# A feed-forward block by one level of Strassen, its weights prepared in seven pieces, and a planner with new figures

## The chip, the core and the metric

The kernel runs on one core of a Trainium2 chip. The core has a matrix engine (TensorE, PE in the profile, with its weight loads as PEld), a vector engine (VectorE, DVE), a scalar engine (ScalarE, ACT), a general engine (GpSimd, POOL) and a queue that starts most transfers (SyncE, SP). The metric is the time of one execution on the device in microseconds; lower is better.

## What is computed

Three layers stand behind each other, for 2304 tokens (4 sequences of 576) of width 512:

```python
# attention, 8 heads of width 64, seq 576, a bias from the positions
scores = q @ k.T / sqrt(64) + bias          # bias: a small two-layer net on log distances
attn = exp(scores - max); attn = attn / sum
x = attn @ v                                 # (2304, 512)
# first feed-forward, 512 -> 2048 -> 512
h = x @ w_in;  x = (s * relu(h)**2 + b) @ w_out
# second feed-forward, 512 -> 2048 -> 512
h = x @ w_in2; out = (h - tanh(h)) @ w_out2
```

The feed-forward weights arrive as 64-bit floats.

## The kernel before

Every operand of a large product is scaled by a power of two and split into two 16-bit floats, a high part and a low part. A product is then three matmuls (high by high, high by low, low by high) that add up in PSUM. Making a high part is one scaled copy (line 488 on VectorE or line 490 on ScalarE), a low part one scalar_tensor_tensor on VectorE (line 493). A 64-bit weight first becomes a 32-bit float by three integer operations on VectorE (lines 1101, 1104 and 1107), on pieces of 128 by 1024.

The attention runs in 144 units of 128 query rows by 576 keys: scores on TensorE (line 911), bias and maximum on VectorE (943), exp on ScalarE (953), high part (965 or 963), low part on GpSimd (971), a transposing DMA, and the product with the values (990, 996). The first feed-forward takes the tokens in 9 blocks of 256: 16 chunks of hidden units (1406), relu and square on ScalarE, high part (1429) on VectorE, low part on GpSimd (1433), then the output product (1475) into a single PSUM bank that is emptied (1489, 1494) before the next column group can start. It is mixed with the attention on TensorE's queue and goes on after the attention's end.

Once the last transposed attention output is stored, the attention's memory is freed (the task `turn`), and the weights of the second feed-forward are loaded through two staging buffers (`w2raw`), converted, and split into `w2big`. The second feed-forward takes a first block of 256 tokens and four of 512: for each of 16 hidden chunks twelve matmuls (`pg`, 1707), tanh on ScalarE (1715), h - tanh on VectorE (1719), high part (1726) and low part (493) on VectorE, then for each of four output columns 48 matmuls (`pq`, 1755), a scaled copy on ScalarE (1767), and a store.

The order on each engine's queue is fixed when the program is built. A planner (`Schedule`) plays the tasks through with a cost for each task and engine, takes for each free engine the task with the lowest due number among those that can start, and where a task has several engines, the one it comes to first. The table `SHIFT` moves the due numbers of groups of tasks.

## Time and profile before

| | |
|---|---|
| runs | 1095.21, 1097.35, 1097.79 us; median 1097.35 |
| profiled execution: span from the first to the last instruction | 1094.4 us |
| the runs' median less the span, the part that lies around it | 2.95 us |
| TensorE busy | 993.5 us (91%), 9231 matmuls |
| VectorE busy | 735.4 us (67%), 1551 instructions |
| ScalarE busy | 554.1 us (51%) |
| GpSimd busy | 339.1 us (31%) |
| mean granted TensorE clock | 0.964 of 2.4 GHz |

The page gives the profiled execution's span; its own time is taken as that span and the 2.95 us. Busy times of one engine are ends of instructions less their starts, and neighbours overlap a little, so the pace of an engine is read from start to start. A matmul's shown duration holds its way through the array as well; its pace, too, is the distance between starts.

### The profile page before, as it was taken

The page shows a single profiled execution, that of the slowest core. Times are in us where ns is not written, and L with a number is a line of the kernel's source. Part 1 is how long each engine was busy: PE and PEld are TensorE (multiplying, and loading weights), DVE is VectorE, ACT ScalarE, POOL GpSimd, SP SyncE. Part 2 cuts the span into 40 slices and gives each one's busy share as a digit, 9 for nine tenths or more (in the row PEclk, how much of TensorE's full clock was granted, in tenths as well). Part 3 has the DMA queues.
Part 4 walks back from the last instruction along what each step waited for, and adds up shares of the span by engine and source line. Part 5 has one row for each costly group of instructions (what it writes and reads, how often), then busy time and mean ns, then how long its engine had stood idle before and what let it go on. Part 6 is the DMA issues. An engine that isn't in the chain of part 4 may idle for free. (4 is left out here: it accounts for less than half of the span.)

```text
span 1094.4 us, 23536 instructions
## 1 busy us (share of the span) xinstructions
PE 993.5 (91%) x9231; PEld 668.8 (61%) x9234; DVE 735.4 (67%) x1551; ACT 554.1 (51%) x1120; POOL 339.1 (31%) x371
## 2 busy tenths in 40 slices
PE   6547677999998899999999999999999999999998
PEld 3113245678787677878778788887454444444443
DVE  6999999945677686877773689998852487016200
ACT  6898878768776665665655365631220122102100
POOL 6035346545475375656744041400000000000000
PEclk9767888999999999999999999999999999999999
DMA  9979996799999799999896644412000000000000
GB/s 342 369 209 233 252 264 114 179 234 220 245 169 220 157 219 182 191 157 195 156 180 118 205 146 169 159 54 92 1 5 20 20 1 1 20 20 6 15 29 29
DMA packets 250368, 153.10 MB, mean 140 GB/s; under 512 B 197392, under 2 KB 216464, under 8 KB 250256
## 3 DMA queue, kind: packets, MB, share of 16 engines
q1 hardware_dynamic: 250256, 151.59, 58.3%
q8 instruction: 72, 1.18, 0.5%
q14 instruction: 40, 0.33, 0.1%
...
## 5 line engine op out<-in xcount | busy, mean ns | idle before, releaser
L971 POOL TENSOR_TENSOR hl<-e,hl 128x64 f16<-128x64 f32 (+1 forms) x288 | 230.2, 821 | 240.9 <-ACT hl L965 145.0
L1475 PE MATMUL po<-hr,w1big 128*128 128x256 f16 x1728 | 202.4, 273 | 11.2 <-ACT x L1494 7.7
L1755 PE MATMUL pq<-w1big,w2big 128*128 128x512 f16 (+1 forms) x960 | 189.5, 358 | 0.0
L1475 PEld LDWEIGHTS <-w1big 128*128 128x128 f16 x1728 | 165.7, 98 | 35.3 <-issue 16.5
L1406 PEld LDWEIGHTS <-w1big 128*128 128x128 f16 x1728 | 165.8, 99 | 31.4 <-issue 11.7
L1707 PE MATMUL pg<-hr,w2big 128*128 128x512 f16 x768 | 168.0, 379 | 0.0
L1755 PEld LDWEIGHTS <-w2big 128*128 128x128 f16 x960 | 93.8, 98 | 92.6
L1707 PEld LDWEIGHTS <-w2big 128*128 128x128 f16 x960 | 93.8, 98 | 92.5
L953 ACT ACTIVATE e<-sp,mx 128x576 f32<-128x576 f32 x144 | 105.5, 733 | 57.6 <-DVE mx L947 37.0
L943 DVE CUSTOM_DVE_ANT_0 sp<-sp,bi 128x576 f32<-128x576 f32 x144 | 109.7, 761 | 33.9 <-PE sp L911 24.3
L1433 POOL TENSOR_TENSOR hr<-r,hr 128x512 f16<-128x512 f32 x72 | 93.3, 1297 | 117.8 <-DVE hr L1429 106.0
L1715 ACT ACTIVATE t<-pg,ich 128x512 f32<-128x512 f32 (+1 forms) x80 | 51.4, 644 | 142.7 <-PE pg L1707 136.8
L1719 DVE SCALAR_TENSOR_TENSOR t<-pg,ich,t 128x512 f32<-128x512 f32 (+1 forms) x80 | 55.2, 695 | 100.1 <-ACT t L1715 99.8
L1406 PE MATMUL ph<-xt_own,w1big 128*128 128x256 f16 x960 | 115.2, 276 | 3.8 <-DMA xt_own<-xh 2.3
L911 PE MATMUL sp<-ks,qs 64*128 64x288 f16 (+1 forms) x960 | 83.4, 298 | 24.4 <-ACT e L953 22.7
L1767 ACT ACTIVATE o<-pq,osc 128x512 f32<-128x512 f32 (+1 forms) x20 | 12.9, 644 | 161.8 <-PE pq L1755 161.8
L1406 PE MATMUL ph<-w1big 128*128 128x256 f16 x768 | 89.1, 274 | 0.0
L965 ACT ACTIVATE hl<-e 128x576 f16<-128x576 f32 x110 | 74.7, 679 | 24.1 <-DMA et<-hl 22.2
L911 PEld LDWEIGHTS <-qs 64*128 64x128 f16 (+1 forms) x960 | 47.5, 100 | 49.9 <-issue 37.5
L990 PEld LDWEIGHTS <-et 128*128 128x128 f16 (+1 forms) x1440 | 54.3, 103 | 36.8 <-issue 20.2
L990 PE MATMUL xp<-vp,et 128*128 128x64 f16 (+1 forms) x1440 | 65.1, 198 | 12.3 <-DMA et<-hl 8.8
L1429 DVE CAST hr<-r 128x512 f16<-128x512 f32 x72 | 41.2, 574 | 29.2 <-ACT r L1424 24.3
...
## 6 DMA issues: line engine op xcount, KB each, us to landing
...
```

The costliest lines, as they stand in the source:

```text
L911: nc.tensor.matmul(out=out, lhsT=qs.tile[64 * h:64 * h + 64, sq, p * r:p * r + r], rhs=ks.tile[64 * h:64 * h + 64, sk, half * HS:(half + 1 ...
L943: nc.vector.tensor_tensor_reduce(out=st, in0=st, in1=bi.tile.rearrange("p (a b) -> p a b", a=2), scale=-1.0 / KAP, scalar=3.0e38, op0=ALU. ...
L953: nc.scalar.activation(out=put(e, row_tile("e")).rearrange("p (a b) -> p a b", a=2), in_=sp.tile[:, :, 0:HS], func=AF.Exp, scale=-1.0, bia ...
L965: nc.scalar.activation(out=h[:, 0:S], in_=e.tile, func=AF.Copy)
L971: nc.gpsimd.tensor_tensor(out=hl.tile[:, o:o + m], in0=e.tile[:, c:c + m], in1=hl.tile[:, c:c + m], op=ALU.subtract)
L990: nc.tensor.matmul(out=xp[r0:r0 + r, o:o + 64], lhsT=et.tile[:, n, r0:r0 + r], rhs=vp.tile[:, 0, n % 5, 64 * h:64 * h + 64], start=n == 0, ...
L1406: nc.tensor.matmul(out=ph.tile[:, fi, :], lhsT=win_ap(1, sw, m, f), rhs=xa(sx, m), start=m == 0 and j == 0, stop=m == KM - 1 and j == 2,)
L1433: nc.gpsimd.tensor_tensor(out=rh[:, :, 1, :], in0=r.tile, in1=rh[:, :, 0, :], op=ALU.subtract)
L1475: nc.tensor.matmul(out=po.tile[:, :NB1], lhsT=wout_ap(1, sw, f, c), rhs=rhl[f // 8][:, f % 8, sr, :], start=f == 0 and j == 0, stop=f == K ...
L1707: nc.tensor.matmul(out=pg.tile[:, :n], lhsT=win_ap(2, sw, m, f), rhs=xh[:, sx, m, :n], start=m == 0 and i == 0, stop=m == KM - 1 and i == 2,)
L1719: nc.vector.scalar_tensor_tensor(out=tt.tile[:, :n], in0=pg.tile[:, :n], scalar=xs2[j][1], in1=tt.tile[:, :n], op0=ALU.mult, op1=ALU.subtract,
L1755: nc.tensor.matmul(out=pq.tile[:, :n], lhsT=wout_ap(2, sw, f, c), rhs=g[:, sr, :n], start=f == 0 and i == 0, stop=f == KF - 1 and i == 2,)
```

## The change

The second feed-forward is computed by one level of Strassen's method (in the form with seven products and fifteen sums). Tokens are in 9 blocks of 256, the 2048 hidden units in two slices of 1024, so there are 18 rounds `k`. In each round, the input product (128 + 128 tokens, 256 + 256 input columns, 512 + 512 hidden units) takes seven products `in_product(k, p)` and the output product seven `out_product(k, p)`, each of 24 matmuls with a 128-wide moving operand and a weight load each, where plain blocks would take eight. The sums are formed on VectorE: on the weights (`wsum`, line 1753), on the block's input (`xsum`, 1820), on the hidden values (`add`, `combine`; 1968 to 2031) and on the output (2091 to 2137). High and low parts are now needed for seven sums where there were four quarters. The tables `ONLY` and `opts` keep all of these off GpSimd.

The weights are loaded into seven staging places that are later overwritten, are converted at once (eight pieces of the input weights, then eight of the output weights, four of these in two halves of 128 by 512), and are then split; before, conversion, splitting and the first block's work were mixed. The planner gets other costs per task, another rule for VectorE beside GpSimd, other costs for transfers, and a new `SHIFT`, so that every queue's order is new, in the attention as well. In the attention, 49 of the 144 high parts stand on VectorE (before 34) and 95 on ScalarE (before 110).

```diff
--- before
+++ after
+EARLY, E0, EP = 0, 40, 50
-AHEAD = 3.4
+AHEAD = 6.0
+COST = {
+    "u.ex@act": 1.056, "u.hi@act": 1.132, "bias.lambda@act": 1.102, "f.relu@act": 0.952, "f.square@act": 1.145,
...
+}
+PORT = {"u.ttr": 0.0, "x.scale": 0.0, "scan.add": 0.0, "k.lambda": 0.4, "v.lambda": 0.4, "q.lambda": 0.4, "s.lambda": 0.4,
...
+}
+ONLY = {"I.fn": "dve", "I.sub": "dve", "J.fn": "dve", "J.c22": "dve", "I.add": "dve", "X.xsum": "dve", "P.wsum": "dve", "u.lo": "pool", "f.lo": "pool"}
-    ".begin": -153, ".identity": -9.52, ".fn": -349.02, ".lambda": 99.24, "scan0.lambda": -15.42, "scan0.fn":
...
+    ".begin": -932.5, ".fn": 1185, ".lambda": 1257, "I0.add": -102.8, "I0.fn": -1616, "I0.lambda": -1827.5,
...
-    HOP = 0.23
-    PACE = dict(pe=1.0, act=1.02, dve=1.06, pool=1.0)
-    DMA_START, DMA_DONE = 0.65, 2.0
+    HOP = dict(pe=0.22, act=0.07, dve=0.07, pool=0.1, turn=0.0)
+    LATE = dict(act=0.034, dve=0.034, pool=0.034)
+    OVER = dict(act=0.1, dve=0.085, pool=0.04)
+    DMA_START, DMA_DONE = 1.2, 0.65
+    SHARE, SHARE_POOL, SHARE_MAX = 0.65, 0.18, 2.1
...
+                if eng == "dve" and t.share > 0.0:
+                    rest = port["pool"] - at
+                    if rest > 0.0:
+                        cost = min(cost + t.share * rest, cost * self.SHARE_MAX)
+                        late("pool", self.SHARE_POOL * min(rest, cost))
+                    port["dve"], user["dve"] = at + cost, t
+                elif eng == "pool":
+                    rest = min(port["dve"] - at, cost)
+                    if rest > 0.0:
+                        cost += self.SHARE_POOL * rest
+                        late("dve", user["dve"].share * rest)
+                    port["pool"], user["pool"] = at + cost, t
+                free[eng] = at + max(cost - self.OVER[eng], 0.06)
+                t.end = at + cost + self.LATE[eng]
...
-    def w2_f32(i):
-        return (big2[0][:, i + 1, :] if i < 7 else w1big[:, 5, :]).bitcast(F32)
-
...
+    PC = 2048
+    ORD_IN, ORD_OUT = (1, 2, 5, 6, 3, 7, 4), (1, 5, 2, 3, 7, 6, 4)
+    XSLOT = {1: 0, 2: 1, 3: 3, 4: 6, 5: 4, 6: 5, 7: 2}
+    HT = NB1 // 2
...
+    def w2_late(i, j, deps, prio, dest=()):
...
+        if g == 0:
+            bufs = [lambda: flat2(big2[0][:, 2 * n % 14:2 * n % 14 + 2, :]).bitcast(U32)]
+        elif n % 2 == 0:
+            bufs = [lambda: w1big[:, 5, :].bitcast(U32)]
+        else:
+            bufs = [lambda: f_pc(22).bitcast(U32), lambda: xt_own[:, 1, :].bitcast(U32)]
+        war = [x for x in t_stage.get((g, n - (2 if g else 7)), [])]
...
+    def w2_split(g, s, deps, prio):
+
+        sc.tag = f"P{g}{s}"
+        i1, i2 = 4 * g + s, 4 * g + s + 2
+        if g == 0:
+            q = {11: (i1, 0), 12: (i1, 1), 21: (i2, 0), 22: (i2, 1)}
+        else:
+            q = {11: (i1, 0), 12: (i2, 0), 21: (i1, 1), 22: (i2, 1)}
+        raw = {k: (lambda v=v: raw2(*v)) for k, v in q.items()}
+
+        def split(p, src, deps, o):
+            dst = lambda part: prod_w(g, s, p)[:, part].rearrange("p a n -> p (a n)")
+            th = sc.add(
+                {ACT: 1.14}, lambda e: copy_scale(dst(0), src(), w2s["c", g], e), deps + [t_w2c[g]], prio + o
+            )
+            tl = sc.add({DVE: 1.28}, lambda _: low_part(dst(1), src(), w2s["c", g], dst(0)), [th], prio + o + 0.5)
+            t_wp[g, s, p] = [th, tl]
+            return [th, tl]
+
+        def combine(out, a, b, op, deps, o):
+            def wsum(e):
+                (nc.gpsimd if e == POOL else nc.vector).tensor_tensor(out=out(), in0=a(), in1=b(), op=op)
+            return [sc.add({POOL: 2.5, DVE: 1.21}, wsum, deps, prio + o)]
+        a22 = split(4, raw[22], deps, 0)
+        a11 = split(1, raw[11], deps, 1)
+        a12 = split(2, raw[12], deps, 2)
+        s1 = combine(raw[22], raw[21], raw[22], ALU.add, a22, 0)
+        split(5, raw[22], deps + s1, 3)
+        s3 = combine(raw[21], raw[11], raw[21], ALU.subtract, s1, 1)
+        split(7, raw[21], deps + s3, 5)
+        s2 = combine(raw[11], raw[22], raw[11], ALU.subtract, s3 + a11, 1)
+        split(6, raw[11], deps + s2, 4)
+        s4 = combine(raw[12], raw[12], raw[11], ALU.subtract, s2 + a12, 2)
+        split(3, raw[12], deps + s4, 6)
+        return [x for p in PRODS for x in t_wp[g, s, p]]
...
+        def combine(out, i, j, op, deps):
+            def xsum(e):
+                x = x_raw()
+                (nc.gpsimd if e == POOL else nc.vector).tensor_tensor(out=x[:, out], in0=x[:, i], in1=x[:, j], op=op)
+            return sc.add({POOL: 0.95, DVE: 0.37}, xsum, deps, prio)
+        t1 = combine(4, 2, 0, ALU.subtract, lds + [t])
+        t3 = combine(2, 3, 2, ALU.subtract, [t1])
+        t2 = combine(5, 3, 4, ALU.subtract, [t1])
...
+    def in_product(k, p):
...
+            w = prod_w(0, s, p)
+            xs = y()[:, :, XSLOT[p]].rearrange("p s (m n) -> p s m n", m=2)
+            for f in range(4):
+                for m in range(2):
                     for i, (sw, sx) in enumerate(((0, 0), (0, 1), (1, 0))):
                         nc.tensor.matmul(
-                            out=pg.tile[:, :n], lhsT=win_ap(2, sw, m, f), rhs=xh[:, sx, m, :n],
-                            start=m == 0 and i == 0, stop=m == KM - 1 and i == 2,
+                            out=bank.tile[:, f * HT:(f + 1) * HT], lhsT=w[:, sw, m, f * 128:(f + 1) * 128], rhs=xs[:, sx, m],
...
+        def split(n, q):
+            i = st["G", n]
+            dst = lambda part: g_mem[k % 2]()[:, (q - 1) * 1024 + part * 512:(q - 1) * 1024 + part * 512 + 512]
+            war = [t_prod["out", k - 2, q]] if k >= 2 else moe1_end if k == 0 else out_done[1]
+            o = pr + 100 + 10 * ORD_OUT.index(q)
+            th = sc.add(
+                {ACT: 0.72, DVE: 0.49}, lambda e: copy_scale(dst(0), i.tile, names["cg"], e), [st["tG", n]] + war, o, [], [i]
+            )
...
+        if p == 1:
+            copy("E1", bank)
+        elif p == 2:
+            gate(11, st["E1"], [from_psum("E1", bank)])
+            split(11, 1)
+        elif p == 5:
+            copy("E5", bank)
+        elif p == 6:
+            copy("E2", bank)
+        elif p == 3:
+            gate(12, st["E2"], [from_psum("E2", bank)])
+            combine("T1", 12, 11)
+            split("T1", 5)
+        elif p == 7:
+            copy("E3", bank)
+            e3, e5 = st["E3"], st["E5"]
+
+            def add(e):
+                eng_of(e).tensor_tensor(out=e3.tile, in0=e3.tile, in1=e5.tile, op=ALU.add)
+            tc22 = sc.add(dual(add), add, [st["t", "E3"], st["t", "E5"]], pr, [], [e3, e5])
+            gate(22, e3, [tc22])
+            combine("T3", 22, 12)
+            combine("T2", 22, "T1")
+            split(22, 3)
+            split("T3", 7)
+            split("T2", 6)
+        else:
+            gate(21, bank, [t], True)
+            combine("T4", 21, "T2")
+            split(21, 2)
+            split("T4", 4)
+
+    accs = {}
+
...
+    def out_product(k, p):
...
+            w = prod_w(1, s, p)
+            g = g_mem[k % 2]()[:, (p - 1) * 1024:p * 1024].rearrange("p (s k n) -> p s k n", s=2, k=4)
+            o = (j % 2) * 256
+            for f in range(4):
+                for c in range(2):
+                    for i, (sw, sx) in enumerate(((0, 0), (0, 1), (1, 0))):
+                        nc.tensor.matmul(
+                            out=bank.tile[:, o + c * HT:o + (c + 1) * HT], lhsT=w[:, sw, f, c * 128:(c + 1) * 128],
+                            rhs=g[:, sx, f], start=new and f == 0 and c == 0 and i == 0,
+                            stop=s == 1 and f == 3 and i == 2, skip_group_check=True,
+                        )
...
+    NS = 2 * NB2
+    for k in range(NS + 1):
+        if k < NS and k % 2 == 0 and k // 2 + 1 < NB2:
+            pass
+        ins = [(in_product, k, p) for p in ORD_IN] if k < NS else []
+        outs = [(out_product, k - 1, p) for p in ORD_OUT] if k else []
+        order = ins
+        if ins and outs:
+            order = ins[:3] + outs[:1] + ins[3:4] + outs[1:2] + ins[4:5] + outs[2:3] + ins[5:6] + outs[3:5] + ins[6:] + outs[5:]
+        elif outs:
+            order = outs
+        for fn, kk, p in order:
+            fn(kk, p)
+        if k % 2 == 0 and k // 2 + 1 < NB2:
+            prep_tasks(k // 2 + 1, 1e4 + 200 * (k + 1) - 300)
     sc.run()
 
```

VectorE's queue around the first block of the second feed-forward. `xs`/`am` (before) and `cols` (after) belong to that block's scales, `hr<-r` to the first feed-forward, `w2raw` is a staging buffer; in the new order `w1big` and `xt_own` are staging, too. Before:

```order
L1107 SCALAR_TENSOR_TENSOR w2big<-w2raw,w2big 128x1024
L1608 TENSOR_REDUCE am<-xs 128x4
L1615 TENSOR_REDUCE sx<-am 128x1
L1616 TENSOR_TENSOR am<-am,w2r_ic 128x4
L1617 TENSOR_REDUCE sx<-am 128x1
L493 SCALAR_TENSOR_TENSOR w2big<-w2big,w_c 128x1024
```

After:

```order
L1178 SCALAR_TENSOR_TENSOR w2big<-w1big,w2big 128x1024
L1500 CAST hr<-r 128x2x256
L1172 TENSOR_SCALAR w2big<-w2big 128x512
L1172 TENSOR_SCALAR w2big<-xt_own 128x512
L1175 SCALAR_TENSOR_TENSOR w2big<-w2big 128x512
L1175 SCALAR_TENSOR_TENSOR w2big<-xt_own,w2big 128x512
L1178 SCALAR_TENSOR_TENSOR w2big<-w2big 128x512
L1500 CAST hr<-r 128x2x256
L1178 SCALAR_TENSOR_TENSOR w2big<-xt_own,w2big 128x512
L1788 TENSOR_REDUCE cols<-w1big 128x8
```

Before, the block's first reduction stood behind 9 of the 16 conversions and ahead of all splitting; now it stands behind all 16 conversions and behind the splits and sums of all the input weights.

The same queue a little later, behind that block's low parts (`w1big<-w2big,w_c,w1big` is a low part of an output weight, L1753 a sum of weights, `pb` a PSUM bank of the first round). After:

```order
L563 SCALAR_TENSOR_TENSOR w1big<-w1big,cols 128x1280
L563 SCALAR_TENSOR_TENSOR w1big<-w2big,w_c,w1big 128x1024 x2
L1753 TENSOR_TENSOR w2big<-w2big 128x1024
L563 SCALAR_TENSOR_TENSOR w1big<-w2big,w_c,w1big 128x1024
L1753 TENSOR_TENSOR w2big<-w2big 128x1024
L563 SCALAR_TENSOR_TENSOR w1big<-w2big,w_c,w1big 128x1024
L1753 TENSOR_TENSOR w2big<-w2big 128x1024
L563 SCALAR_TENSOR_TENSOR w1big<-w2big,w_c,w1big 128x1024
L1753 TENSOR_TENSOR w2big<-w2big 128x1024
L563 SCALAR_TENSOR_TENSOR w1big<-w2big,w_c,w1big 128x1024
L1968 SCALAR_TENSOR_TENSOR w2big<-pb,cols,w2big 128x512
L563 SCALAR_TENSOR_TENSOR w1big<-w2big,w_c,w1big 128x1024
```

The first round's first result from PSUM (L1968) is taken in between the output weights' low parts; before, the first block's hidden values were worked off in between conversions.

TensorE's queue where the second feed-forward begins (`po` is the first feed-forward's output, `pg` and `pa` hidden values of the second). Before:

```order
L1475 LDWEIGHTS w1big
L1475 MATMUL po<-hr,w1big 128x256
L1707 LDWEIGHTS w2big
L1707 MATMUL pg<-xt_own,w2big 128x256
```

After:

```order
L1546 LDWEIGHTS w1big
L1546 MATMUL po<-hr,w1big 128x256
L1942 LDWEIGHTS w2big
L1942 MATMUL pa<-w1big,w2big 128x128
```

Each matmul has a weight load of its own in both. Before, the first `pg` stood behind 636 of the 1068 matmuls of the first feed-forward that follow the attention's last product; now the first `pa` stands behind 1080 of 1176; 108 of these matmuls, which stood ahead of the attention's last product, stand behind it now.

## Rows read from the trace of the kernel before

**Rows 1.** Busy time by stage; columns: stretch, length, each engine's busy time (instructions), clock, DMA

```profile
core 0: us, PE busy (x) PEld busy (x) DVE busy (x) ACT busy (x) POOL busy (x), PEclk, DMA share, GB/s
27.00:220.00 193.00, 133.36 (x1350) 74.44 (x1351) 184.30 (x353) 160.10 (x309) 79.75 (x80) 0.81 0.89 231
220.00:591.00 371.00, 349.80 (x4684) 290.53 (x4684) 255.63 (x696) 245.37 (x542) 210.51 (x260) 1.00 0.98 191
591.00:640.00 49.00, 46.43 (x445) 41.23 (x438) 27.04 (x41) 23.17 (x52) 10.14 (x10) 1.00 0.52 170
640.00:740.00 100.00, 96.47 (x878) 85.51 (x877) 95.36 (x154) 51.80 (x106) 21.60 (x13) 1.00 0.38 130
740.00:1094.00 354.00, 350.58 (x1712) 166.98 (x1709) 155.44 (x267) 56.63 (x84) 0.00 (x0) 1.00 0.06 20
```

**Rows 2.** Chain that ended last, in order of time; columns: start, length, what

```profile
716.36 5.24 PE po L1475 x48
...
756.20 41.44 PE pg L1707 x192
...
1090.62 0.03 ACTq L1767
```

**Rows 3.** Groups of instructions by line and shape; busy time, mean ns, idle before

```profile
L1707 PE MATMUL pg<-hr,w2big 128*128 128x512 f16 x768 | 168.0, 379 | 0.0
L1755 PE MATMUL pq<-w1big,w2big 128*128 128x512 f16 x768 | 167.9, 379 | 0.0
...
L1707 PEld LDWEIGHTS <-w2big 128*128 128x128 f16 x960 | 93.8, 98 | 92.5
...
L1707 PE MATMUL pg<-xt_own,w2big 128*128 128x256 f16 x192 | 22.1, 273 | 0.0
```

**Rows 4.** TensorE's timeline, narrow matmuls at full clock; start, length, line, count

```profile
13.86 1.21 PE L738 MATMUL gram<-w1big 128*128 128x128 bf16 x18
14.99 0.71 PE L631 MATMUL pb<-hr,cst_sb 128*32 128x512 f32 x3
...
562.77 0.44 PE L990 MATMUL xp<-vp,et 128*128 128x64 f16 x9
563.04 0.31 PE L996 MATMUL xp<-vp,et 128*128 128x64 f16 x5
```

**Rows 5.** TensorE's timeline behind the attention's last product

```profile
591.33 11.96 PE L1406 MATMUL ph<-w1big 128*128 128x256 f16 x108
...
609.42 5.40 PE L1475 MATMUL po<-hr,w1big 128*128 128x256 f16 x48 [0.78 <-ACT x L1494]
```

**Rows 6.** VectorE's timeline, conversions and splits of the second feed-forward's weights

```profile
605.14 0.69 DVE L1101 TENSOR_SCALAR w2big<-w2raw 128x1024 uint32<-128x1024 uint32 x1
605.87 2.06 DVE L1104 SCALAR_TENSOR_TENSOR w2big<-w2raw,w2big 128x1024 uint32<-128x1024 uint32 x1
...
665.43 0.68 DVE L1101 TENSOR_SCALAR w2big<-w2raw 128x1024 uint32<-128x1024 uint32 x1
666.15 1.22 DVE L1104 SCALAR_TENSOR_TENSOR w2big<-w2raw,w2big 128x1024 uint32<-128x1024 uint32 x1
...
668.55 1.28 DVE L493 SCALAR_TENSOR_TENSOR w2big<-w2big,w_c 128x1024 f16<-128x1024 f32 x1
...
722.66 2.47 DVE L493 SCALAR_TENSOR_TENSOR w2big<-w2big,w_c 128x1024 f16<-128x1024 f32 x2
```

**Rows 7.** VectorE's timeline, pace of smaller instructions

```profile
591.44 0.42 DVE L1036 TENSOR_TENSOR xf<-xp,sum 128x256 f32<-128x256 f32 x1 [1.35 <-PE xp L996]
...
656.95 1.21 DVE L1608 TENSOR_REDUCE am<-xs 128x4 f32<-128x1024 f32 x1
...
983.88 0.48 DVE L1726 TENSOR_SCALAR w1big<-t,cg 128x512 f16<-128x512 f32 x1
984.28 0.74 DVE L1719 SCALAR_TENSOR_TENSOR t<-pg,ich,t 128x512 f32<-128x512 f32 x1
984.94 0.74 DVE L493 SCALAR_TENSOR_TENSOR w1big<-t,cg,w1big 128x512 f16<-128x512 f32 x1
```

608 lines of the change are left out of this document (397 added, 211 removed), and 187 rows, old and new, of the table SHIFT.

## The prediction

> **What bounds the kernel now.** The table by stage comes first [rows 1]. While the attention starts (27 to 220 us) VectorE is busy 184.3 of 193 us and TensorE 133.4, at a granted clock of 0.81; from 220 on TensorE is the busy engine at a clock of 1.00: 349.8 of 371 us, 46.4 of 49, 96.5 of 100, and 350.6 of 354 in the second feed-forward, where VectorE has 155.4 and ScalarE 56.6. The chain that ended last [rows 2] is TensorE from 716 us to 1090.62, matmul behind matmul, and then 3.8 us to the span's end at 1094.4 (last copy and store). So from the attention's end on, a matmul that goes is worth its own duration, until VectorE, which has to make the sums, comes late. Third, I read paces, from start to start: 192 of 512 columns take 41.44 us, 215.8 ns each; 48 of 256 take 5.24, 109.2 ns [rows 2]; narrower ones stand in the timeline [rows 4]: nine of 64 columns start 0.27 us ahead of the next group (30.0 ns), 18 of 128 take 1.13 us up to the next instruction (62.8 ns with that handover). The attention's last product ends at 591.3 [rows 5]; the first conversion of a second-layer weight starts 13.8 us behind it [rows 6].
>
> **Products.** Removed are 768 + 768 matmuls of 512 columns and 192 of 256 [rows 3] with as many in the output product: 1536 × 0.2158 = 331.5, 384 × 0.1092 = 41.9, together 373.4 us. Added are 18 × 14 = 252 products of 24, 6048 matmuls of 128 columns, each with a weight load. No long stream of these is in the trace. Below, half of a 256-column one, 54.6 ns: 330.2 us. Above, the 18-matmul group with its handover, 62.8: 379.8. A line through the paces at 64, 256 and 512 columns gives 30.0, 109.2 and 215.8 nearly exactly, and 56.4 at 128; I take it: 1.354 us a product, 341.1 us. The products alone thus give −32.3 us (ends −43.2 and +6.4). Weight loads cost nothing in this, because the pairs at 64 and 256 columns carry one each too; their shown 98 ns [rows 3] overlap.
>
> **The seam.** In the new order 108 matmuls of the first feed-forward move from ahead of the attention's last product to behind it: at 0.1092 [rows 2] that is 11.8 us, which I put down as the attention's end at 591.3 − 11.8 = 579.5, first conversion at 593.3. TensorE then has 1080 matmuls, 117.9 us, and the waits that this stretch has before, 2.6 + 3.5 = 6.1 us of idle time [rows 1]: the first product of the second layer could start at 703.5. VectorE, from the first conversion to that block's operand: 16 conversions at 665.43 to 668.55, 3.12 us [rows 6] = 49.9; 14 low parts of 1024 at 1.2 (2.47 for two, [rows 6]) = 16.8; 8 weight sums of 1024 at 1.2 (no such sum is in the trace; a reduction of as many elements takes 1.21, [rows 7]) = 9.6; some 20 casts of the first layer at 0.40 [rows 7] = 8; the block's reduction, sums and low parts 8; small instructions 4; and 12 for GpSimd's company, which makes a conversion's step 2.06 instead of 1.22 [rows 6]. Sum 108.3: at 701.6, so the start isn't late, by 2 us. Behind it, ahead of or among the first round's work, stand the output weights' 14 low parts (16.8) and 8 sums (9.6), the next block's preparation (6.0) and the round's own share, 12.2: 44.6, thus 746.2. The first round's output products and the second round's last input product wait for that queue; with two products behind it that one ends at 748.9. Unstalled, it is the 19th product: 579.5 + 1176 × 0.1092 + 6.1 + 19 × 1.354 = 739.7. I take a wait of 9 us; bounds 0 and 28 (if the attention does not end earlier, and VectorE's instructions wait 5%).
>
> The remaining 233 products take 315.5, the tail 3.8 as before: 748.9 + 315.5 + 3.8 = 1068.2 us of span; with the 2.95 around it 1071.1. The profiled execution of before has 1094.4 + 2.95 = 1097.35 by the same counting, the median of the runs; so the forecast is 26 us less. Of the 32.3 from the products the wait at the seam takes 9; the 11.8 at the attention only move work, since the moved matmuls come back; and the 3.4 us of idle time that the last 354 us have now [rows 1] are not carried over.
>
> **Rounds.** A round of 14 products is 18.95 us of TensorE. VectorE has in it 3 results from PSUM, 8 sums and 7 low parts of 512 at 0.66 (984.28 to 984.94, [rows 7]) = 11.9; some high parts 0.5; 3.5 output sums of 256 at 0.42 [rows 7] = 1.5; half a block's preparation (four sums 1.7, a reduction 1.2, low parts 2.3) = 2.6; some nine small ones, taken at half of the 256-element one, 1.7. Sum 18.2. That is 96% of TensorE's round: hidden, by little. ScalarE: 14 instructions a round at the 0.67 that 84 of them take now in 56.6 us [rows 1] is 9.4, half. The moved high parts in the attention are 15 × 0.40 = 6 us on VectorE; they lie beside TensorE's 349.8 and cost nothing as long as VectorE's 255.6 of 371 [rows 1] leaves room.
>
> **The attention's order.** By counts the same work in a new order. TensorE's idle time there is 21.2 us in 220 to 591 and 59.6 in 27 to 220 [rows 1]. I take nothing beyond the move above, with 20 us to either side as bounds (the idle time of the later stretch, won or doubled).
>
> **Rivals.**
> 1. The seam never makes TensorE wait: GpSimd has less for VectorE to suffer from. Then 739.7 + 315.5 + 3.8 + 2.95 = 1062. For it speaks that the wait is the small difference of two long sums. Chance 0.15.
> 2. VectorE becomes the bound of the rounds, and the kernel slower. Each sum waits for the one before and for PSUM, and its queue is served in order, so that one late result delays the next product's operand. The gain of 26 us over 16 rounds is 1.6 us a round: the sign turns at 20.6 us on VectorE, 13% above my 18.2. At 22 us the kernel takes 1071 + 16 × (22 − 18.95) = 1120. For it: 96% leaves no slack, and the small instructions are not in the rows; against it: now 512-wide instructions do follow each other at 0.66 without gaps [rows 7], and GpSimd, which stretches them, has nothing to do there (0.00 us, [rows 1]). Chance 0.20, of which 0.09 ends faster still (up to 20 us a round), 0.02 equal, 0.09 slower.
> 3. A 128-wide matmul doesn't cover its weight load. At the shown 98 ns a pair [rows 3], 6048 of them take 592.7 instead of 341.1: some 1320. The groups of [rows 4] speak against it: 62.8 ns with a load each, and even 64-wide ones go at 30. Chance 0.03. A milder form of the same stands in the Trainium skill (TensorE: Matmul & The Clock Gate, section Back-to-back issue gap): a sustained stream of load and matmul at 128 columns is given there as about 81 ns a matmul, and 56 for an isolated one. By that the products would take 6048 × 81 = 489.9 us and the kernel an estimated 1071 + 148.8 × 233/252 = 1209; I give this form 0.02 of the 0.03. The trace disagrees so far: for 512 columns the same section gives 131, and the rows show 215.8, and its 18 narrow pairs go at 62.8 at most; but 18 are no long stream.
> 4. The attention comes out longer by the new order, for example because VectorE, the bound until 220 us, gets the 15 high parts there. Price up to 20 or 30 us: 1091 to 1101, middle 1095. For it: a busy share of 95% in that stretch [rows 1]; against it: they add 6 us at most. Chance 0.10, half of it faster still, 0.02 equal, 0.03 slower.
>
> **How the numbers follow.** Forecast 0.52, with its own range 1058 to 1084 (pace 54.6 is −10 us, a seam wait of 20 is +11). It and the first rival are faster, 0.67; with 0.09 and 0.05 of the others 0.81, and rounding for what I don't see, 0.80. Equal (within 0.3%, 3.3 us, about the spread of the three runs) 0.05; slower 0.09 + 0.03 + 0.03 = 0.15. The range reaches down to 1046 (no wait, 54.6 ns, and a few us from the attention) and up to 1100, beyond which lie the slower half of rival 2 and rival 3.
>
> **What would show it.** Right: products of 24 at 1.33 to 1.38 us in an unbroken TensorE timeline; the attention's last product at about 579; the first product of the second layer at about 704 and the second round's last input product near 749; VectorE at 17.5 to 19 us per round and TensorE idle under 2% from 750 on; a tail of about 3.8 us. Wrong: TensorE waiting for VectorE in each round (rival 2), a pace above 63 ns (rival 3), an attention that ends after 591.

## The result, and the profile after

The changed kernel takes 1086.65 us (median of 4 runs, 1083.76 to 1089.93) against 1097.28 for the kernel before: a ratio of 0.9908, interval 0.9888 to 0.9927. A second set of four (e12 in the table below) gave 1086.25, ratio 0.9913 (0.9886 to 0.9939). So it is faster by about 10.6 us where the forecast said 26.

The table by stage of the changed kernel, with the columns of [rows 1]:

```profile
27.00:220.00 193.00, 145.59 (x1508) 81.71 (x1504) 178.56 (x370) 158.07 (x312) 83.81 (x84) 0.77 0.91 237
220.00:591.00 371.00, 341.20 (x4544) 279.83 (x4541) 252.64 (x679) 240.06 (x540) 207.54 (x253) 0.99 0.94 188
591.00:640.00 49.00, 42.79 (x359) 36.35 (x357) 37.93 (x59) 25.01 (x56) 12.92 (x8) 0.93 0.61 226
640.00:740.00 100.00, 93.07 (x900) 82.48 (x898) 92.04 (x143) 61.40 (x106) 26.20 (x16) 0.98 0.26 86
740.00:800.00 60.00, 54.10 (x887) 53.98 (x887) 59.06 (x100) 38.34 (x55) 0.00 (x0) 0.91 0.08 24
800.00:900.00 100.00, 100.00 (x1789) 100.00 (x1787) 95.66 (x213) 54.70 (x83) 0.00 (x0) 1.00 0.10 31
```

From 800 us on nothing is lost: TensorE is busy all the time at a granted clock of 1.00. What is lost lies ahead of it. From 591 to 800 TensorE has 190.0 of 209 us, and its clock is below 1.00 in all three stretches, where the kernel before had 1.00 throughout. The clock is not the same each time: in a second profile of the same kernel (e12) it is 1.00 up to 740 us, and 0.94 behind that. Two rows of that profile:

```profile
591.00:640.00 49.00, 43.67 (x397) 38.47 (x395) 40.72 (x61) 28.02 (x59) 13.74 (x8) 1.00 0.60 227
740.00:800.00 60.00, 55.07 (x940) 54.74 (x938) 59.59 (x107) 37.40 (x55) 0.00 (x0) 0.94 0.09 27
```

TensorE's timeline of the changed kernel at the seam (start, length, line, count, and in brackets the idle time before with what ended it):

```profile
582.50 0.33 PE L1067 MATMUL xp<-vp,et 128*64 128x64 f16 x10
...
613.02 0.81 PE L1546 MATMUL po<-hr,w1big 128*128 128x256 f16 x6 [1.88 <-POOL hr L1504]
615.45 1.16 PE L1546 MATMUL po<-hr,w1big 128*128 128x256 f16 x5 [1.61 <-POOL hr L1504]
...
617.50 7.76 PE L1546 MATMUL po<-hr,w1big 128*128 128x256 f16 x48 [0.68 <-ACT x L1565]
...
720.87 1.50 PE L1942 MATMUL pa<-w1big,w2big 128*128 128x128 f16 x24
...
741.89 4.43 PE L1942 MATMUL pa<-w1big,w2big 128*128 128x128 f16 x48 [2.20 <-ACT w1big L1961]
...
753.07 2.61 PE L2070 MATMUL acc<-hr,w1big 128*128 128x128 f16 x23 [4.01 <-DVE hr L563]
...
766.50 1.50 PE L1942 MATMUL pa<-w1big,w2big 128*128 128x128 f16 x24
```

The attention's last product ends at 582.8, the first product of the second layer starts at 720.87, and the 19th product ends at 767.8. The new waits are those for GpSimd's low parts (line 1504) in the first feed-forward's tail, one for a copy of ScalarE, and 4.01 us for the first low part of hidden values (line 563). Behind these waits TensorE runs slower here, at a mean granted clock of 0.93 between 591 and 640 us: 48 matmuls take 7.76 us at 617.50, and 5.40 where the clock is 1.00 [rows 5].

Two rows of waits, TensorE for the attention's transposing transfers between 27 and 580 us (total, times, longest), of the changed kernel and of the one before:

```profile
PE xp L1061 <- DMA et<-hl: 35.6, 33, 3.4
```

```profile
PE xp L990 <- DMA et<-hl: 7.2, 11, 3.0
```

The rounds: busy times of TensorE, its weight loads, VectorE, ScalarE and GpSimd from the 20th product to the last but one:

```profile
768.00:1080.00 312.00, 312.00 (x5581) 312.00 (x5579) 279.21 (x554) 163.62 (x247) 0.00 (x0) 1.00 0.08 26
```

5581 matmuls in 312 us are 55.9 ns each, 1.342 a product; VectorE's 279.2 are 16.8 us per round of 18.8, or 89% of it.

So the sum's own terms, beside this profiled execution (1087.81 us for a span of 1086.0):

| term | forecast | measured | difference |
|---|---|---|---|
| attention's last product ends | 579.5 | 582.8 | +3.3 |
| from there to the first new product | 124.0 | 138.1 | +14.1 |
| from there to the end of the 19th product | 45.4 | 47.0 | +1.6 |
| 233 products | 315.5 | 313.6 | -1.9 |
| tail | 3.8 | 4.6 | +0.8 |
| around the span | 2.95 | 1.8 | -1.1 |
| sum | 1071.1 | 1087.8 | +16.8 |

The attention's end moves from run to run by itself. In the eleven profiles that share the new order up to there (the changed kernel, twice, and nine of the experiments) it lies between 582.8 and 591.6, mean 586.4; in three with the old order at 588.4, 590.6 and 591.3, mean 590.1. The end came 3.7 us earlier on average, not 11.8. The first term is thus +7 rather than +3.3 in the mean; the second is 134.0 to 138.1 in the five profiles with the same tail (mean 135.2), which is +11 in the mean. The third is 45.7 us in the second profile (e12), so it too moves by more than a microsecond.

### The profile page after: what moved, and what is told of

Its sections match the earlier page's. It is cut to its first block, busy times and chain, and to the rows that moved or that the text cites. A ratio compares the mean times of both kernels' runs of the same rounds, so it can differ in the third digit from the quotient of the medians.

```text
span 1086.0 us, 32355 instructions
## 1 busy us (share of the span) xinstructions
PE 974.0 (90%) x13370; PEld 823.4 (76%) x13370; DVE 888.1 (82%) x1881; ACT 685.5 (63%) x1313; POOL 345.7 (32%) x370
## 4 chain that ended last, share of the span: by engine, by line
PE 52%; DVE 16%; DMA 14%; ACT 7%; issue 5%; POOL 4%; SPq 2%; DVEq 0%; ACTq 0%; POOLq 0%
PE acc L2070 13%; PE po L1546 10%; DMA et<-hl 10%; PE pa L1942 9%; PE pb L1942 6%; PE ph L1477 6%; POOL hl L1042 2%; DVE sp L1013 2%; PE po L2070 2%; PE sp L981 2%; POOL hr L1504 2%; PE xp L1061 2%; DVE w1big L1175 1%; ACT e L1023 1%; DVE hr L1500 1%
## 5 line engine op out<-in xcount | busy, mean ns | idle before, releaser
L1546 PE MATMUL po<-hr,w1big 128*128 128x256 f16 x1728 | 208.5, 277 | 12.4 <-POOL hr L1504 4.8
L1546 PEld LDWEIGHTS <-w1big 128*128 128x128 f16 x1728 | 167.7, 100 | 40.4 <-issue 18.9
L1477 PEld LDWEIGHTS <-w1big 128*128 128x128 f16 x1728 | 166.6, 99 | 25.8 <-issue 6.1
L1942 PEld LDWEIGHTS <-w2big 128*128 128x128 f16 x3024 | 175.7, 99 | 2.4 <-issue 2.3
L2070 PEld LDWEIGHTS <-w1big 128*128 128x128 f16 x3024 | 174.2, 98 | 4.1 <-issue 4.1
L1013 DVE CUSTOM_DVE_ANT_0 sp<-sp,bi 128x576 f32<-128x576 f32 x144 | 109.6, 761 | 45.4 <-PE sp L981 34.0
L1504 POOL TENSOR_TENSOR hr<-r,hr 128x512 f16<-128x512 f32 x72 | 99.1, 1378 | 126.1 <-DVE hr L1500 118.0
L1061 PE MATMUL xp<-vp,et 128*128 128x64 f16 (+1 forms) x1440 | 65.4, 198 | 37.5 <-DMA et<-hl 35.6
L2070 PE MATMUL acc<-hr,w1big 128*128 128x128 f16 x1296 | 81.5, 221 | 4.0 <-DVE hr L563 4.0
L1035 ACT ACTIVATE hl<-e 128x576 f16<-128x576 f32 x95 | 64.7, 682 | 24.6 <-DMA et<-hl 23.3
L2070 PE MATMUL acc<-w2big,w1big 128*128 128x128 f16 x1296 | 79.0, 219 | 0.0
L981 PEld LDWEIGHTS <-qs 64*128 64x128 f16 (+1 forms) x960 | 45.7, 101 | 33.8 <-issue 21.1
L1490 ACT ACTIVATE r<-ph 128x512 f32<-128x512 f32 x72 | 42.5, 592 | 37.6 <-PE ph L1477 30.0
L1942 PE MATMUL pa<-w1big,w2big 128*128 128x128 f16 x960 | 62.8, 224 | 2.2 <-ACT w1big L1961 2.2
L1495 ACT ACTIVATE r<-r,sq 128x512 f32<-128x512 f32 x72 | 51.7, 720 | 1.1
```

The lines of the kernel that those rows point to most:

```text
L981: nc.tensor.matmul(out=out, lhsT=qs.tile[64 * h:64 * h + 64, sq, p * r:p * r + r], rhs=ks.tile[64 * h:64 * h + 64, sk, half * HS:(half + 1 ...
L1013: nc.vector.tensor_tensor_reduce(out=st, in0=st, in1=bi.tile.rearrange("p (a b) -> p a b", a=2), scale=-1.0 / KAP, scalar=3.0e38, op0=ALU. ...
L1035: nc.scalar.activation(out=h[:, 0:S], in_=e.tile, func=AF.Copy)
L1061: nc.tensor.matmul(out=xp[r0:r0 + r, o:o + 64], lhsT=et.tile[:, n, r0:r0 + r], rhs=vp.tile[:, 0, n % 5, 64 * h:64 * h + 64], start=n == 0, ...
L1477: nc.tensor.matmul(out=ph.tile[:, fi, :], lhsT=win_ap(1, sw, m, f), rhs=xa(sx, m), start=m == 0 and j == 0, stop=m == KM - 1 and j == 2,)
L1504: (nc.gpsimd if e == POOL else nc.vector).tensor_tensor(out=rh[:, :, 1, :], in0=r.tile, in1=rh[:, :, 0, :], op=ALU.subtract)
```

## The experiments

All ratios are to the kernel before, timed beside; "changed" is 0.9908 to 0.9913.

| | what | median us | ratio | interval |
|---|---|---|---|---|
| e12 | changed, a second time | 1086.25 | 0.9913 | 0.9886 to 0.9939 |
| e1 | two of three conversion operations out | 1080.19 | 0.9851 | 0.9828 to 0.9874 |
| e2 | GpSimd's low parts out, from block 7 | 1078.85 | 0.9835 | 0.9809 to 0.9861 |
| e3 | 174 matmuls in the waits | 1087.69 | 0.9925 | 0.9899 to 0.9952 |
| e4 | changed, attention in the old order | 1097.36 | 1.0006 | 0.9990 to 1.0022 |
| e5 | before, attention in the new order | 1108.03 | 1.0100 | 1.0074 to 1.0125 |
| e6 | low parts on VectorE, from block 7 | 1082.29 | 0.9864 | 0.9845 to 0.9884 |
| e7 | as e6, high parts on ScalarE | 1080.97 | 0.9858 | 0.9833 to 0.9882 |
| e6b | only high parts on ScalarE | 1087.03 | 0.9913 | 0.9898 to 0.9928 |
| e8 | seven weight low parts out | 1087.39 | 0.9912 | 0.9898 to 0.9927 |
| e9 | e7, attention in the old order | 1085.92 | 0.9904 | 0.9884 to 0.9925 |
| e10 | 4 more sums a round | 1123.25 | 1.0257 | 1.0219 to 1.0295 |
| e11 | changed, shorter transposes | 1063.00 | 0.9698 | 0.9676 to 0.9721 |
| e14 | before, shorter transposes | 1087.64 | 0.9920 | 0.9906 to 0.9935 |
| e13 | before, 110 matmuls fewer in the attention | 1094.81 | 0.9996 | 0.9985 to 1.0006 |
| e15 | changed, 110 matmuls fewer in the attention | 1085.86 | 0.9910 | 0.9894 to 0.9927 |

### e1 and e2: who holds up the first feed-forward's tail

```diff
-    lambda _, c=c, o=o, buf=buf: conv_steps(buf(), raw2(i, j)[:, o * m:(o + 1) * m])[c](_),
+    lambda _, c=c, o=o, buf=buf: conv_steps(buf(), raw2(i, j)[:, o * m:(o + 1) * m])[c](_) if c == 0 else None,
```

> The changed kernel, with the second and third integer operation of every second-layer weight conversion left out (so these weights are not the right ones): VectorE loses 16 x 2.4 = 39 us between the attention's end and the first round, the order on all queues stays. Theory A, VectorE's conversions hold up both the first feed-forward's last blocks (casts queue behind them, GpSimd's low parts are stretched) and the first round: the 135.5 us from the attention's end to the first new product fall to about 126, the 47 us from there to the end of the 19th product to about 39, the time from 1086.7 to 1068-1074. Rival B, the handover of the single output bank and the order of the first feed-forward set the stretch: 1082 or more. Rival C, the missing time lies ahead of the attention's end: 1082 or more, and the stretch itself as before.

```diff
             def lo(e, rh=rh, r=r):
+                if n >= 6:
+                    return
                 (nc.gpsimd if e == POOL else nc.vector).tensor_tensor(
```

> The changed kernel, with GpSimd's low parts of the first feed-forward's hidden values left out from its seventh block on (so the result of these blocks lacks a term); VectorE keeps all its work, and without GpSimd beside it its conversions are not stretched. Theory A1, GpSimd's slow low parts (2.07 us beside the conversions against 1.16) are what TensorE waits for in two places behind the attention: these waits (4.8 us) and the slow clock behind them go, 1086.7 becomes 1074-1079. Rival A2, VectorE's casts are late by themselves, behind two or three conversions each: TensorE waits for the casts instead, 1082 or more.

TensorE's timeline of e1, then of e2, at the places shown above:

```profile
585.74 0.33 PE L1067 MATMUL xp<-vp,et 128*64 128x64 f16 x10
...
609.59 5.40 PE L1546 MATMUL po<-hr,w1big 128*128 128x256 f16 x48
...
711.81 1.50 PE L1942 MATMUL pa<-w1big,w2big 128*128 128x128 f16 x24
...
743.28 2.61 PE L2070 MATMUL acc<-hr,w1big 128*128 128x128 f16 x23 [4.88 <-DVE hr L563]
```

```profile
589.51 0.33 PE L1067 MATMUL xp<-vp,et 128*64 128x64 f16 x10
...
613.36 5.40 PE L1548 MATMUL po<-hr,w1big 128*128 128x256 f16 x48
...
715.58 1.50 PE L1944 MATMUL pa<-w1big,w2big 128*128 128x128 f16 x24
...
747.06 2.61 PE L2072 MATMUL acc<-hr,w1big 128*128 128x128 f16 x23 [4.88 <-DVE hr L563]
```

From the last attention product's end to the first new product both take 125.8 us, where the changed kernel has 134 to 138: the 48 matmuls go through without a break, whichever of the two neighbours is lightened. So the loss there needs both, VectorE's conversions and GpSimd's low parts side by side. In time e1 is some 6 us and e2 some 8 us faster than the changed kernel; e2 lies in its theory's range. The wait of 4.9 us in the first round stays in both, also with some 39 us less on VectorE: theory A was right about the stretch and wrong for that place, and its total (1068 to 1074) is too low, mostly for that reason.

### e6, e7 and e6b: GpSimd too slow, or its casts too late

```diff
+FORCED = """0d 1s 45d 8d 2s 3s 4s 5s 9s 7d 13s 11s 15s 6d 82d 83a 84o 20s 85d 89a 90a 10p 91d 92a 22s 86p 24s 334s 93p 87a
...
+2285p 2281a 1819s 2282a 2286p 2283d 2284d 2291p 2504t 2505s 2287a 2511s 2288a 2292p 2289d 2517s 2290d 2297p
...
+FORCED = [(int(x[:-1]), dict(p="pe", a="act", d="dve", o="pool", s="sp", t="turn")[x[-1]]) for x in FORCED.split()]
```

The planner follows the changed kernel's own sequence of tasks, given as task numbers with a letter for the engine; in e6 the 24 low parts of the seventh to ninth block (2284 is the first of them) have `d`, VectorE, in place of `o`, GpSimd. In e7 the casts ("hi") of the same blocks are ScalarE copies as well, and in e6b only these are.

> The changed kernel with one thing moved: the low parts of the first feed-forward's hidden values go from GpSimd to VectorE from the seventh block on, at the same place of the order (24 of them behind the attention). Theory A1, GpSimd beside VectorE is what costs the 12 us behind the attention: the stretch from the last attention product to the first new product falls from 138 to 126-129 us, although VectorE gets 24 x 0.66 = 16 us more; the time is 1077-1081. Rival A2, VectorE's queue is the limit there and the added 16 us come out at the first round: 1084-1092.

> As the kernel with the low parts on VectorE from the seventh block on, and the high parts (casts) of the same blocks on ScalarE, so that VectorE's work behind the attention grows by 24 x (0.66 - 0.40) = 6 us only. Theory A1: the same 126 us for the stretch, and a first round no later: 1074-1079. Rival, ScalarE's queue (25 of 49 and 61 of 100 us busy) makes the high parts late: 1082-1090.

> The changed kernel with only the high parts (casts) of the first feed-forward's hidden values moved from VectorE to ScalarE, from the seventh block on; the low parts stay on GpSimd. Theory A2, the low parts are late because the casts ahead of them queue behind two or three conversions and come in bunches: the stretch behind the attention falls to 126-129 us, the time to 1076-1081. Theory A1, GpSimd beside VectorE's conversions is too slow by itself (2.07 us each) and slows these: 1083-1087, waits for the low parts stay.

The stretch is 128.6 us in e6 (584.6 to 713.17), 127.0 in e7 and 132.6 in e6b. The times of e6 and e7 lie 1 to 2 us above theory A1's ranges. With the casts on ScalarE (e6b) the waits for GpSimd go down to 0.5 us, but the time stays that of the changed kernel. TensorE's waits from 585 to 740, for the single output bank's copies and for GpSimd, in the changed kernel and in e6b:

```profile
PE po L1546 <- POOL hr L1504: 4.8, 3, 1.9
PE po L1546 <- ACT x L1565: 4.3, 5, 0.9
```

```profile
PE po L1767 <- ACT x L1786: 4.9, 5, 1.4
...
PE po L1767 <- POOL hr L1725: 0.5, 1, 0.5
```

So neither theory of e6b holds in full: the stretch does not fall to A2's 126 to 129 us, and the waits for the low parts do not stay, as A1 has it. Against the changed kernel's mean of 135.2, taking GpSimd out of the stretch gives 7 to 8 us, taking only the casts off VectorE 3. The two engines in the changed kernel, first GpSimd's low parts, then VectorE:

```profile
590.17 1.15 POOL L1504 TENSOR_TENSOR hr<-r,hr 128x512 f16<-128x512 f32 x1 [13.61 <-DVE hr L1500]
...
603.70 2.07 POOL L1504 TENSOR_TENSOR hr<-r,hr 128x512 f16<-128x512 f32 x1 [0.96 <-DVE hr L1500]
```

```profile
598.29 0.69 DVE L1172 TENSOR_SCALAR w2big<-w2big 128x1024 uint32<-128x1024 uint32 x1 [2.96 <-DMA w2big<-in_win]
...
604.67 1.64 DVE L1172 TENSOR_SCALAR w2big<-w2big 128x1024 uint32<-128x1024 uint32 x1
...
611.88 1.37 DVE L1500 CAST hr<-r 128x512 f16<-128x512 f32 x1
```

The same low part takes 1.15 us alone and 2.07 beside the conversions; the same conversion operation 0.69 alone and 1.64 beside GpSimd. The second and third operation of a conversion (lines 1175 and 1178, on 1024 columns) take 1.21 to 1.23 us in this trace, beside GpSimd as well. Over the whole stretch the 24 low parts take 39.9 us on GpSimd, 12 more than at 1.15 each. e7 is the fastest kernel here that computes everything: its interval lies below that of the changed kernel.

### e3 and e8: the first round, and the clock

```diff
+WARM = dict(po={1189: 30, 1195: -24, 1387: 20}, i={144: 36}, o={1: -64})
...
+        m = WARM[kind].get(q, 0)
...
+        for _ in range(abs(m)):
+            nc.tensor.matmul(out=warm_t[0][:, :128], lhsT=ones16, rhs=ones16, start=True, stop=True)
```

> The changed kernel, with 174 matmuls of 128 columns on a constant tile put in front of five matmuls that wait behind the attention's end (30, 24, 20, 36 and 64 of them; they fill 1.7, 1.3, 1.1, 2.0 and 3.6 us of waits of 1.9, 1.6, 1.3, 2.2 and 4.0 us); the waits themselves stay, all results too. Theory D, about half of the missing time is TensorE at 1.2 GHz behind each of these waits: the granted clock between 591 and 800 us stays at 1.00 and the time falls by 5 to 8 us, to 1079-1082. Rival: the clock falls for another reason or the waits grow: within 2 us of 1086.7.

The rows by stage of e3:

```profile
591.00:640.00 49.00, 46.37 (x451) 41.50 (x449) 40.58 (x61) 27.88 (x60) 13.76 (x8) 1.00 0.61 227
740.00:800.00 60.00, 56.67 (x1002) 56.04 (x999) 59.60 (x103) 38.32 (x56) 0.00 (x0) 1.00 0.08 24
```

The granted clock is 1.00 in both, as theory D has it, where the two profiles of the changed kernel have 0.93 and 1.00, and 0.91 and 0.94; but the time did not fall (1087.69). In the profile the stretch behind the attention is 135.6 us, and from the first new product to the 19th's end it is 45.5: both lie where the changed kernel's own profiles have them (134.0 to 138.1, and 45.7 and 47.0). TensorE still waits for VectorE behind the added matmuls, and once more one product later, as its timeline of e3 shows:

```profile
752.14 1.44 PE L2085 MATMUL acc<-hr,w1big 128*128 128x128 f16 x23 [1.30 <-DVE hr L564]
...
755.96 0.22 PE L2085 MATMUL acc<-hr,w1big 128*128 128x128 f16 x1 [1.03 <-ACT hr L561]
```

So the slow clock was not the cause: in the first round TensorE was ahead of VectorE anyway.

```diff
-    tl = sc.add({DVE: 1.28}, lambda _: low_part(...), [th], prio + o + 0.5)
+    tl = sc.add({DVE: 1.28}, lambda _: None if g + s == 2 else low_part(...), [th], prio + o + 0.5)
```

> The changed kernel without the seven low parts of the output weights' second half, which VectorE makes behind the first feed-forward's last matmul (so half of the output products lack a term): 7 x 1.2 = 8.4 us less on VectorE between 739 and 754 us, where the first low part of the hidden values stands behind them. Theory G, these hold the first round up: the wait of 4.0-4.9 us at its first output product and the slow clock behind it go; 1079-1082. Rival H, the first round's own chain of results, tanh, sums and splits is that long: the wait stays, 1085-1088.

TensorE's timeline of e8 at the first output products:

```profile
725.58 1.50 PE L1942 MATMUL pa<-w1big,w2big 128*128 128x128 f16 x24
...
751.96 1.65 PE L2070 MATMUL acc<-hr,w1big 128*128 128x128 f16 x24
...
756.84 0.22 PE L2070 MATMUL acc<-hr,w1big 128*128 128x128 f16 x1 [1.89 <-ACT hr L560]
```

The first output product no longer waits, so theory G named the right instructions: they stand on VectorE ahead of the first low part of hidden values, and can't start before the first feed-forward's last matmul frees their memory. But half of the wait comes back one product later; the 19th product ends 43.0 us behind the first instead of 45.7 and 47.0. The median shows none of these 3 to 4 us: it lies in rival H's range (the profile has the attention's end at 591.6, the latest of all); that such a gain is in the time as well is not shown.

### e4, e5 and e9: the attention's order by itself

The planner of one kernel is made to follow the other's sequence of tasks and engines up to the attention's end, and goes on by itself behind that (in e9, by the changed kernel's own sequence).

```diff
+            if total - n < len(FORCED):
+                seq, eng = FORCED[total - n]
+                t = self.tasks[seq]
...
+            else:
+                best = None
+                for eng in ENGINES:
```

> The changed kernel, but up to the attention's end every task is issued in the order and on the engine that the kernel before had; behind it the new planner goes on. 108 more matmuls of the first feed-forward stand ahead of the attention's end again. Theory E, the new attention order loses about 6 us by itself (585.4 instead of 579.5): the attention ends at 591, 96 fewer matmuls stand behind it, and the time is 1080-1084. Rival F, the new order costs nothing, its difference is the clock of single runs, and VectorE's later start of the conversions has less first feed-forward to hide behind: 1087-1095.

> The kernel before (two plain feed-forwards), but up to the attention's end every task is issued in the order and on the engine that the changed kernel has; behind it its own planner goes on. Theory E, the changed attention order loses time by itself: the attention ends at 584-588 with 108 fewer matmuls of the first feed-forward done, where 579.5 would be even, and the time is 1101-1107 against 1097. Rival F, the new order costs nothing: the attention ends at 578-581 and the time is 1094-1099.

> The changed kernel in another order: up to the attention's end every task as the kernel before had it, behind that all that is left in the changed kernel's own order, with the first feed-forward's high parts on ScalarE and low parts on VectorE from the seventh block on (GpSimd has nothing behind the attention). Theory: the attention order of before is about 8 us shorter at equal work, and without GpSimd VectorE's conversions and splits are done some 118 us behind the attention's end (13.8 + 104), as TensorE is (111 + 6): first new product at 706-710, time 1070-1077. Rival: with 108 fewer matmuls behind the attention VectorE's work is the limit, the first product waits for it or the first rounds do: 1082-1092.

TensorE's timeline of e5 at the attention's end, and its waits for the transposing transfers from 27 to 580 us:

```profile
586.87 0.33 PE L1131 MATMUL xp<-vp,et 128*64 128x64 f16 x10
```

```profile
PE xp L1125 <- DMA et<-hl: 33.0, 29, 3.5
```

e5 is theory E: the kernel before with the new attention order has 108 matmuls less ahead of the attention's end, yet that comes only 4.2 us earlier; 7.6 of 11.8 us are lost, and the time is 11.0 us longer, 1 us beyond theory E's range. e4 and e9, which should have won this back, didn't: e9's time is its rival's, and 5 us longer than that of e7, which differs from it in the attention's order. In e4 theory E was right about the attention (its end is at 588.4 with 108 more matmuls done) and wrong about the total; rival F names why, though the median is 2 us above its range. The profile of e4 is that of the fastest of its ten runs, 1091.92 us. TensorE's timeline of e4 behind the attention:

```profile
588.16 0.33 PE L1204 MATMUL xp<-vp,et 128*64 128x64 f16 x10
...
719.80 1.50 PE L2079 MATMUL pa<-w1big,w2big 128*128 128x128 f16 x24
...
739.10 5.28 PE L2079 MATMUL pa<-w1big,w2big 128*128 128x128 f16 x48 [3.56 <-ACT w1big L2098]
...
769.22 0.26 PE L2079 MATMUL pb<-w2big 128*128 128x128 f16 x1 [3.12 <-ACT w2big L697]
```

VectorE's preparation can start only with the attention's end, and with fewer matmuls to cover it TensorE waits: the stretch to the first new product is still 131.4 us, with 60 matmuls (6.6 us) fewer in it, and the first two rounds wait more. In e9, where GpSimd is out of the way, the stretch is 129.6 us, with 108 matmuls fewer than in e7, which has 127.0. In the changed kernel the 108 moved matmuls are not lost; they cover conversions.

### e11, e13, e14 and e15: what paces the attention

```diff
+            if u < 16:
+                nc.sync.dma_start_transpose(out=o, in_=hl.tile)
+            else:
+                nc.sync.dma_start_transpose(out=o[:, 0:5], in_=hl.tile[:, 0:640])
...
-                        out=xp[r0:r0 + r, o:o + 64], lhsT=et.tile[:, n, r0:r0 + r],
+                        out=xp[r0:r0 + r, o:o + 64], lhsT=et.tile[:, n - 5 if n > 4 and u >= 16 else n, r0:r0 + r],
```

> The changed kernel with the attention's transposing transfers cut to 5 of their 9 blocks from the 17th unit on (TensorE makes all its products, but the second half of a low part's blocks with the high part's data, so the result is off); every queue's order stays. Theory J, in the new order the attention is paced by these transfers (the 16 DMA engines are busy 0.94-0.98 of the time from 220 to 580 us): TensorE's waits for them, 35 us in the profile, fall below 12, the attention ends at 570-578 instead of 582-591, the time is 1072-1080. Rival K, the waits come from the order in which scores, exp and splits are issued: the waits stay above 25 us and the time is 1084 or more.

> The kernel before, with the transposing transfers cut to 5 of 9 blocks from the 17th unit on, as was done to the changed kernel (where it gave 23 us). Theory J1, in the old order TensorE and the transfers are near balance, only the 7 us of waits for them are to be had: the attention ends at 583-588, 1089-1094. Theory J2, the transfers set the old order's pace as they do the new one's: the end moves by 15 us or more, below 1083.

```diff
     for j, (sw, sx) in enumerate(((0, 0), (0, 1), (1, 0))):
+        if n == 3 and f < 10 and m + j > 0:
+            continue
         nc.tensor.matmul(
...
-            start=m == 0 and j == 0, stop=m == KM - 1 and j == 2,
+            start=m == 0 and j == 0, stop=(m == KM - 1 and j == 2) or (n == 3 and f < 10),
```

> The kernel before, without 110 of the first feed-forward's input matmuls in the middle of the attention (11 of each 12 of ten chunks in its fourth block, so that block's result is off): 12.0 us less of TensorE, every order stays. The prediction's step, matmuls that leave the attention bring its end forward by their duration: 1085. Theory J, the transposing transfers (16 DMA engines at 0.98 from 220 to 591 us) pace the attention as well: TensorE waits for them instead, the end comes 2-6 us earlier, 1091-1095.

> The changed kernel without the same 110 matmuls in the middle of the attention (12.0 us less of TensorE). The prediction's step: 1074.5. Theory J, the transfers pace the attention: its end stays within 3 us of 582-591, TensorE's waits for the transfers grow from 35-40 to 45 us or more, 1083-1087.

The attention's last product in e11:

```profile
562.11 0.33 PE L1069 MATMUL xp<-vp,et 128*64 128x64 f16 x10
```

The attention ends at 562.4: that is 24 us ahead of the mean of the new order, and the time falls by 23 us, further than theory J's range. The waits for the transfers fall from 35.6 to 17.9 us, not below 12; 13.0 and 12.1 of these fall ahead of 220 us. In e14, the same cut in the old order, the end is at 583.6, 7.7 us earlier, and the time falls by 8, as J1 says, to 1 us below its range. e13 and e15 are the prediction's own step, put to the test: 12.0 us of matmuls leave the attention, and the time changes by 0.9 us in the old order (the interval of its ratio allows 1.6 at most) and by less than 1 in the new. The attention's last product in e13, then in e15:

```profile
588.62 0.33 PE L996 MATMUL xp<-vp,et 128*64 128x64 f16 x10
```

```profile
582.03 0.33 PE L1067 MATMUL xp<-vp,et 128*64 128x64 f16 x10
```

The first end, 588.9, lies among those of the old order, the second, 582.3, half a microsecond ahead of those of the new. In e13 the waits for the transfers rise from 7.2 to 11.2 us, and the granted clock falls in the stretch that has fewer matmuls. In e15 the waits for the transfers do not grow to 45 us, which theory J expected; those of the scores for exp (line 1023) do grow, from 7.7 us in the changed kernel. TensorE's waits in e15 from 27 to 580 us:

```profile
PE xp L1061 <- DMA et<-hl: 36.6, 35, 3.7
PE sp L981 <- ACT e L1023: 16.0, 13, 4.5
```

So both runs show that the matmuls there are worth next to nothing, but in e15 it is not shown that the transfers take up what they leave. The stretch of 300 to 400 us in e13 and in the kernel before:

```profile
300.00:400.00 100.00, 84.85 (x1153) 67.35 (x1150) 72.98 (x177) 67.45 (x138) 56.44 (x67) 0.91 1.01 199
```

```profile
300.00:400.00 100.00, 90.95 (x1244) 74.86 (x1241) 72.84 (x172) 66.24 (x137) 56.29 (x67) 0.98 0.98 193
```

In e13 TensorE has 91 matmuls fewer in it, at a lower clock, and is busy 6.1 us less, and the attention hardly ends earlier: TensorE's busy time is not what sets its pace. The last column but one is the DMA share, 0.98 to 1.01.

### e10: how near VectorE is in the rounds

```diff
     eng_of(e).tensor_tensor(out=home(i), in0=st["G", x].tile, in1=st["G", y].tile, op=ALU.subtract)
+    if n in ('T1', 'T2', 'T3', 'T4'):
+        eng_of(e).tensor_tensor(out=i.tile, in0=st["G", x].tile, in1=st["G", y].tile, op=ALU.subtract)
```

> The changed kernel with each of the four differences of hidden values per round made twice on VectorE (the second one over the first, so the result stays): 4 x 0.6 = 2.4 us more per round of 18.8 us. The prediction's account has VectorE at 18.2 us a round, so it becomes the bound at about 20.6: TensorE waits some 1.8 us per round in 16 rounds and the time goes from 1086.7 to 1110-1125. Rival: its work in a round is less than that account says or is taken up by rounds that have little (every second round has more): below 1100.

The row by stage of e10, 300 us of rounds:

```profile
800.00:1100.00 300.00, 280.04 (x4879) 278.10 (x4877) 283.97 (x543) 142.09 (x214) 0.00 (x0) 0.98 0.08 26
```

2.4 us more a round cost 37 us in all, 2.2 for each of 17 rounds: VectorE is then busy 95%, TensorE 93% and no longer 100%. VectorE's own 16.8 us a round and these 2.4 make 19.2, hardly above 18.8, so it is not the sum of its busy times alone that decides. That the order of results in a round leaves it idle time that can't be used fits this; no run takes it apart. The rounds of the changed kernel have next to no room.

## Why the prediction was wrong, step by step

**Products: right.** 55.9 ns over 5581 matmuls, forecast 56.4. At 128 columns a weight load for each matmul costs nothing that shows. The Trainium skill's figure for a sustained stream of such pairs (TensorE: Matmul & The Clock Gate, section Back-to-back issue gap: about 81 ns) isn't met here: by it the 5581 matmuls would have taken an estimated 452 us instead of 312.

**"108 matmuls ... that is 11.8 us, which I put down as the attention's end at 591.3 − 11.8 = 579.5": failed.** It took TensorE as what ends the attention, because its busy share there was the highest of the engines. The same row had the DMA engines at 0.98 [rows 1], and I passed over that column. e13 and e15 show that matmuls there are worth about nothing, e11 and e14 that shorter transposing transfers are worth 23 us in the new order and 8 in the old. The matmuls moved behind the attention came back there at their full 11.8 us, and ahead of it only 3.7 went: some 8 us, of which 7 show in the sum's first term. With the 11 behind the attention, and some 2 that the table's last terms give back, this is the miss of 16. The sum took nothing for the attention's order, with 20 us to either side as bounds; the 8 lie within these.

**"TensorE then has 1080 matmuls, 117.9 us, and the waits that this stretch has before, 2.6 + 3.5 = 6.1 us": failed.** What it takes beyond the matmuls came to 7.9 us where VectorE or GpSimd was lightened (125.8 us in e1 and e2, less 117.9), and to 16 to 20 in the changed kernel, idle time and slower matmuls together. In the new order conversions follow each other closely on VectorE beside GpSimd's low parts; I had counted 12 us for what GpSimd does to VectorE, and nothing for what VectorE does to GpSimd, whose low parts TensorE waits for: 4.8 us in the changed kernel. Nor is it the step that I named that GpSimd stretches: the operation with 2.06 instead of 1.22 us [rows 6] stays at 1.21 to 1.23 in the changed kernel's trace, and the first operation and the casts grow. This is the other part, 8 to 12 us.

**The seam's wait of 9 us: right in size, by some luck, and half right in cause.** 11.0 us are lost between the first and the 19th product (47.0, or 45.7 in e12, less 96 matmuls of the first layer at 0.1092 and 19 products at 1.341). It is VectorE's queue, but not the whole queue from the first conversion on: with 39 us of conversions out the wait was the same 4.9. It starts with the memory that the first feed-forward's last matmul frees, and with what VectorE then makes out of it (e8).

**Rounds: right in time, too wide in margin.** TensorE doesn't wait, and VectorE has 16.8 us for 18.2 forecast. Rival 2's mechanism is real, since e10 turns the kernel slower, but its price is wrong: with 16.8 + 2.4 = 19.2 us on VectorE its formula gives 16 × (19.2 − 18.95) = 4 us, and 37 were measured, so the sign turns well ahead of the 20.6 us that it names. That the expectation of e10 (1110 to 1125) was met is luck in part: it started from 18.2.

**Rivals.** None of them alone is what happened. Rival 4, the attention, was the nearest, but its price of 20 or 30 us is too high for the 8 found there, and its reason, VectorE's high parts up to 220 us, is not borne out: VectorE is busy 178.6 us there, and was 184.3 before. The transfers were tested, and they count. With the measured 3.7 instead of 11.8 at the attention and 11 us more behind it, the same working gives 1071.1 + 8.1 + 11 = 1090, within 4 us of the medians.

**Open.** Why the new attention order waits five times as long for the same transfers, and why its end scatters by 9 us between profiles of one order, was not taken apart. e11 shows only that their size counts; whether it is the load on the 16 DMA engines or the length of each transfer is open, and so is what takes up the time in e15.
